# Decode attention with a fixed window: the second and third piece of the last values as a wide operand, and the output rows of heads 24 to 27 as 128-wide rows

## The chip, the core and the metric

The kernel runs on one core of a Trainium2 chip. The metric is the device time of one execution in microseconds (us). All times below are in microseconds unless marked ns, and times of events count from the start of the profiled span.

## The reference

Two branches start from the same layer-normed row `x` of 512 numbers. Branch A is one decode step of attention with 32 heads of 128 numbers; each head has keys and values of its own, of which the last 4096 positions are used. Branch B is a small MLP whose result gates branch A.

```python
xn = layernorm(x)
q = (xn @ wq) as 32 heads of 128
k, v = last 4096 positions of k_cache, v_cache       # 32 heads, bf16
p = softmax(q . k * 128 ** -0.5)
o = p @ v                                            # 32 x 128
s = o as 4096 @ wo                                   # 512
out = x + s * silu(B(xn))
```

Keys and values are 32 MB each (32 x 4096 x 128 in bf16), so about 79 MB are read for an output of 512 numbers.

## The kernel before

The heads go in eight groups of `G = 4` (`NG = 8`). A group's keys are one tile `kv` of 4 MB, and so are its values: 128 partitions, of which 32 belong to each head, and on every partition 128 "columns" (`CP`) of 128 numbers, one position each. The main loop runs `s` from 0 to 9. In step `s` it takes the scores of group `s` (part on VectorE, `k_vector`; part on TensorE, `k_turn` and `k_scores`), the softmax of the group before, and the values of group `h = s - 2` (`LAG`). Steps 8 and 9 have no keys any more: step 8 (`s == NG`) finishes the softmax of the last group and does the values of the seventh group; step 9 (the `else`) does the values of the eighth. TensorE, VectorE and ScalarE run in the order in which the code is written (`manual_schedule`). All large loads are issued from one queue in program order (`load`).

The values of a group are weighted in one of two ways:

- *Wide* (`v_wide`, L424): for every four columns one matmul with the 16 weights (4 columns x 4 heads) as the stationary operand and 512 numbers of values as the moving one. Four of these go side by side into four 32-row groups of the PSUM tile `ov`. Then ScalarE copies `ov` to `ov_sb` (L432), four transposes turn it into `ot_ps` (`v_turn`, L443), and VectorE adds up the wanted diagonal blocks into `oT` (`v_add`, L449): 128 numbers for each of the four heads.
- *Narrow* (`v_part`, L460): for each column one matmul with 128 x 128 values as the stationary operand and the four weights as the moving one, straight into `oT`. There is nothing to turn.

The last values arrive in four pieces, columns 0 to 63, 64 to 95, 96 to 111 and 112 to 127 (`cuts`). Behind them in the queue come the rows of `wo` for the last four heads, `wo_rows`, in three pieces: heads 28 and 29, head 30, head 31. In the kernel before, the first piece is wide and is turned at once; the other three are narrow, and add to the `oT` that `v_add` wrote.

`v_out` (L470 for the last groups) multiplies `oT` by the softmax's inverse denominators and gives `o` in bf16. The output projection splits the heads in blocks of 16, 8, 4 and 4. For the first three, `ox_spread` and `ox_pick` rearrange `o` to `ox`, so that a partition holds what fits its rows of `wo`. `y_wide` (L517) multiplies them with 512-wide rows of `wo` into `yr`, in four row groups whose partial sums ScalarE copies to `y_sum` (L640). `rows_add` (L153, its matmul is L156) then sums those into `y_ps`, which holds the 512 outputs as four rows of 128 numbers: it takes one matmul for each row, [...]. The last four heads go directly into `y_ps`, four 128-wide matmuls a head (`y_head`). Last come `y` (L650), `out_row` (L652) and the store.

Of the kernel before, what the change touches and what calls it, by code (L numbers as in the profile page):

```python
# [26 lines left out]
def kernel(  # L27
# [14 lines left out]
    nc = tc.nc  # L42
# [9 lines left out]
    CP = G * W // P  # L52
# [23 lines left out]
    def load(dst, src):  # L76
# [9 lines left out]
                        in_=A_wq.rearrange("(a b c) n -> b a (c n)", a=4, c=KC))  # L86
# [33 lines left out]
    ind = const.tile([P, 1], FP32, name="ind")  # L120
# [32 lines left out]
    def rows_add(ps, col, w, last):  # L153
        k = col.shape[0]
        for j in range(KC):
            nc.tensor.matmul(ps[32 * j:32 * j + 1, :], lhsT=col, rhs=w[0:k, j * P:(j + 1) * P],  # L156
                             start=False, stop=last, skip_group_check=True)
# [46 lines left out]
    for b in range(2):  # L204
        zeros(qr[b][:])
        for c in range(KC):
            wc = wq_sb[:, c, :].rearrange("p (g a d) -> p g a d", a=G, d=Dh)
            for a in range(G):
                nc.tensor.matmul(qr[b][32 * a:32 * a + 1], lhsT=xq_bf[:, c:c + 1], rhs=wc[:, 4 * b:4 * b + 4, a, :],  # L209
                                 start=False, stop=(c == KC - 1), skip_group_check=True)  # L210
    nc.scalar.copy(out=q_row[:, 0:4, 0, :], in_=qr[0][:])
    nc.vector.tensor_copy(out=q_row[:, 4:8, 0, :], in_=qr[1][:])  # L212
    for b in range(2):
        qb_ps = ps_tr.tile([P, 4, Dh], FP32, tag="pt", name="qb_ps")
        nc.tensor.matmul(qb_ps[:], lhsT=sel[:].rearrange("k b a -> k (b a)"), rhs=q_row[:, 4 * b:4 * b + 4, 0, :],
                         start=True, stop=True)
        nc.scalar.copy(out=q_bc[:, 4 * b:4 * b + 4, :], in_=qb_ps[:])
    for b in range(2):
# [5 lines left out]
        for t in range(2):  # L224
            rows = slice(64 * t, 64 * t + 64)
            nc.scalar.copy(out=q_pair[rows, 4 * b:4 * b + 4, :, G * t:G * t + G].rearrange("p g l a -> p g a l"),
                           in_=qt_ps[rows].bitcast(BF16).rearrange("p g (a m l) -> p g a m l", a=G, l=2)[:, :, :, 0, :])
# [4 lines left out]
    for j in range(KC):  # L232
        for c in range(KC):
            nc.tensor.matmul(hs_ps[:, j:j + 1], lhsT=w2_sb[:, c, j::4],
                             rhs=shifted_bf[:, c:c + 1], start=(c == 0), stop=(c == KC - 1))
# [30 lines left out]
    for i in range(11):  # L266
        n = P if i < 10 else 96
        terms.append((a_bf[0:n, i % 3, i // 3:i // 3 + 1], w4_sb[0:n, i, :]))
    for i, (col, w) in enumerate(terms):
        r = 32 * (i % 4)  # L270
        nc.tensor.matmul(hr_ps[r:r + 1].rearrange("r j n -> r (j n)"), lhsT=col, rhs=w, start=False,
                         stop=(i >= len(terms) - 4), skip_group_check=True)
# [124 lines left out]
    def sm_rden(g):  # L397
        s = st[g]
        s["rden"] = sm_pool.tile([P, G], FP32, tag="rden", name="rden")
        nc.vector.reciprocal(out=s["rden"][:], in_=s["den"][:])  # L400
# [20 lines left out]
    ov = ps_o.tile([P, 4, Dh], FP32, name="ov")  # L421
    zeros(ov[:])

    def v_wide(g, v, c1=CP):  # L424
        s = st[g]
        for i in range(c1 // 4):
            c, r = 4 * i, 32 * (i % 4)
            nc.tensor.matmul(ov[r:r + 4 * G], lhsT=s["pT"][:, c:c + 4, :].rearrange("p i a -> p (i a)"),  # L428
                             rhs=v[:, c:c + 4, :], start=(i < 4), stop=(i >= c1 // 4 - 4),
                             skip_group_check=True)  # L430
        s["ov_sb"] = sm_pool.tile([P, 4, Dh], FP32, tag="ov_sb", bufs=2, name="ov_sb")
        nc.scalar.copy(out=s["ov_sb"][:], in_=ov[:])  # L432

    def v_turn(g):
        s = st[g]
        if g == NG - 1:
            ot_ps = ps_tr.tile([P, 4 * P], FP32, tag="pt", name="ot_ps")
        else:
            ot_ps = ps_misc.tile([P, 4 * P], FP32, tag="misc", name="ot_ps")
        s["ot"] = ot_ps  # L440
        step = P - 4
        for j in range(4):
            nc.tensor.transpose(ot_ps[:, step * j:step * j + P], s["ov_sb"][:, j, :], ident_f[:])  # L443
# [13 lines left out]
    def v_part(g, v, c0, c1):  # L457
        s = st[g]
        for c in range(c0, c1):
            nc.tensor.matmul(s["oT"][:], lhsT=v[:, c, :], rhs=s["pT"][:, c, :], start=False,  # L460
                             stop=(c == CP - 1), skip_group_check=True)
# [23 lines left out]
    def ox_pick(i):  # L485
        n = blocks[i][1]
        to, mt, mh = masks[n]
        ox_ps = ps_misc.tile([P, n, n], FP32, tag="misc", name="ox_ps")
        nc.tensor.matmul(ox_ps[:], lhsT=to[:], rhs=ox_blk[i][:], start=True, stop=True)
        pick = sm_pool.tile([P, n, n], FP32, tag="pick", bufs=1, name="pick")  # L490
        nc.vector.tensor_tensor(out=pick[:], in0=ox_ps[:],
                                in1=mh[:].unsqueeze(2).to_broadcast([P, n, n]), op=ALU.mult)
        ox = sm_pool.tile([P, n], BF16, tag=f"ox{n}", bufs=1, name="ox")
        with nc.allow_low_precision("one nonzero addend, a bf16 value"):
            nc.vector.tensor_reduce(out=ox[:], in_=pick[:].rearrange("p h t -> p t h"), axis=AX.X,
                                    op=ALU.add)
        ox_blk[i] = ox
# [15 lines left out]
    def y_wide(i, last):  # L513
        n = blocks[i][1]
        for t in range(n):
            r = 32 * (t % 4)
            nc.tensor.matmul(yr[0][r:r + 1].rearrange("r j n -> r (j n)"), lhsT=ox_blk[i][:, t:t + 1],  # L517
                             rhs=wo_blk[i][:, t, :], start=False, stop=(last and t >= n - 4),
                             skip_group_check=True)

    def y_head(h):
        rows_add(y_ps, o_blk[3][:, h - h_part:h - h_part + 1], wo_row(h), h == H - 1)
# [7 lines left out]
    for s in range(NG + LAG):  # L530
        h = s - LAG
        last = h == NG - 1
        kn = load_kv(k_pool, A_k_cache, s, (0, 64, CP) if s == 0 else (0, CP)) if s < NG else None
        if s == LAG:
            wts_guard.__exit__(None, None, None)
            v_pool = ctx.enter_context(tc.tile_pool(name="v", bufs=V_BUFS))
            wo_blk[2] = v_pool.tile([P, 4, D], BF16, tag="wo_4", bufs=1, name="wo_4")
            wo_rows = v_pool.tile([P, H - h_part, D], BF16, tag="wo_rows", bufs=1, name="wo_rows")
        if last:
            v = load_kv(v_pool, A_v_cache, h, cuts)  # L540
            for r, n in ((H - G, 2), (H - 2, 1), (H - 1, 1)):
                load_rows(r, n)
        elif h >= 0:
            v = load_kv(v_pool, A_v_cache, h)
        if h == 3:
            wo_24 = k_pool.tile([P, 32, D], BF16, tag="kv", name="wo_24")
            wo_blk[0], wo_blk[1] = wo_24[:, 0:16, :], wo_24[:, 16:24, :]
            load_wo(0)
        if h == 5:
            load_wo(1)  # L550
            load_wo(2)

        if s < NG:
            nb = len(batches(s))

            def keys(b0, b1):
                for b in range(b0, b1):
                    k_turn(s, kn, b)
                    if b > 0:
                        k_scores(s, b - 1)  # L560

            k_open(s)
            k_vector(s, kn, 0)
            keys(0, 2)
            if s == 7:
                v_turn(h - 1)
                v_add(h - 1)
                v_out(h - 1)
            elif s > 1:
                sm_den(s - 2)  # L570
                sm_rden(s - 2)
            elif s == 1:
                sm_max(0)
            k_vector(s, kn, 1)
            keys(2, 4)
            if s == 7:
                sm_den(h)
                sm_rden(h)
                keys(4, nb - 2)
                sm_turn(s - 1)  # L580
                keys(nb - 2, nb)
            else:
                if s > 0:
                    sm_turn(s - 1)
                keys(4, nb)
            k_scores(s, nb - 1)
            sm_own(s)
            if s == 7:
                k_vector(s, kn, 2)
                v_wide(h, v)  # L590
                sm_exp(s - 1)
                v_turn(h)
                y_open()
                k_vector(s, kn, 3)
                v_add(h)
                v_out(h)
                ox_spread(1)
                sm_max(s)
                continue
            if s > 0:  # L600
                sm_exp(s - 1)
            if h > 0:
                v_turn(h - 1)
            k_vector(s, kn, 2)
            if h >= 0:
                v_wide(h, v)
            if h > 0:
                v_add(h - 1)
                v_out(h - 1)
            if s == 6:  # L610
                ox_spread(0)
            k_vector(s, kn, 3)
            if s == 6:
                ox_pick(0)
            if s > 0:
                sm_max(s)
        elif s == NG:
            ox_pick(1)
            sm_turn(NG - 1)
            sm_exp(NG - 1)  # L620
            y_wide(1, False)
            sm_den(NG - 2)
            sm_rden(NG - 2)
            y_wide(0, False)
            warm(3)
            v_wide(h, v)
            sm_den(NG - 1)
            sm_rden(NG - 1)
            v_turn(h)
            v_add(h)  # L630
            v_out(h)
            ox_spread(2)
        else:
            v_open(h)
            v_wide(h, v, cuts[1])
            ox_pick(2)
            v_turn(h)
            v_add(h)
            y_wide(2, True)
            nc.scalar.copy(out=y_sum[:], in_=yr[0][:].rearrange("p j n -> p (j n)"))  # L640
            v_part(h, v, cuts[1], cuts[2])
            rows_add(y_ps, ind, y_sum, False)
            for c0, c1 in zip(cuts[2:], cuts[3:]):
                v_part(h, v, c0, c1)
            v_out(h)
            for r in range(H - G, H):
                y_head(r)
# [36 lines left out]
```

## Time and profile before

| | |
|---|---|
| median time of 3 runs | 193.32 (193.32 to 193.47) |
| span of the profiled run | 191.1 |
| mean granted TensorE clock | 0.694 |
| VectorE busy | 150.9 (79% of the span) |
| TensorE matmul busy | 118.9 (62%) |
| ScalarE busy | 89.2 (47%) |
| moved by DMA | 79.02 MB, mean 413 GB/s |

The time is some 2 us longer than the span, which runs from the first to the last instruction. Busy times are sums over the whole span. Steps 8 and 9 are its last 20 us: from about 171 VectorE has no keys left to work on, and what remains are the last values, the output rows and the store.

In the timeline a line gives the start, the duration (first start to last end of what is merged), the engine, the line of code, the operation, what is written from what, shapes and the count; in brackets stands the idle time before it and what ended it. PEld is TensorE's loading of stationary operands. A line of the chain of waits gives start, duration and what the time went to; "issue" is time in which nothing that the profile shows was waited for. The table of stretches gives the busy time of PE, PEld, VectorE, ScalarE and GpSimd, and as its last three numbers the granted TensorE clock as a share of full speed, the busy share of the DMA engines, and GB/s.

### The profile page before, as it was taken

To read this page: it belongs to the slowest core of one execution; us is meant where nothing else is said; L and a number is where in the kernel's file an instruction comes from. 1 tells how busy PE (TensorE), PEld (TensorE's weight loads), DVE (VectorE), ACT (ScalarE), POOL (GpSimd) and SP (SyncE) were. 2 spreads that over 40 slices of the span, in tenths; PEclk is the share of its full clock that TensorE was granted. 3 is DMA by queue.
4 is the path that set the end of the run, shared out by engine and by line. 5 is a ranking of instruction groups with operands and counts; after the bars stand their busy time and mean duration, and the time that the engine had idled before them with its cause. 6 is when DMAs were issued, how large, how long until landed. Compare 5 with 4: busy or idle time off the path is not lost.

```text
span 191.1 us, 2883 instructions
## 1 busy us (share of the span) xinstructions
PE 118.9 (62%) x1180; PEld 76.2 (40%) x1180; DVE 150.9 (79%) x175; ACT 89.2 (47%) x191; POOL 2.3 (1%) x11
## 2 busy tenths in 40 slices
PE   1653854988734368256945773680989189739682
PEld 0430222767523334243434432540863078413351
DVE  1660159979999999999999999999999997990111
ACT  2001370887894076427464564542574147643120
POOL 2110000000000000000000000000000000000000
PEclk9999696555965557955575589558555855996965
DMA  6999999999999999999999999999999998999990
GB/s 211 447 425 413 427 429 429 439 439 430 439 434 439 439 429 425 439 439 432 422 432 425 439 422 408 442 439 435 439 432 441 435 439 372 485 432 387 413 367 26
DMA packets 4732, 79.02 MB, mean 413 GB/s; under 512 B 656, under 2 KB 1264, under 8 KB 1776
## 3 DMA queue, kind: packets, MB, share of 16 engines
q1 hardware_dynamic: 4424, 74.65, 91.5%
q10 hardware_dynamic: 296, 4.20, 5.2%
q8 instruction: 9, 0.15, 0.3%
q14 instruction: 3, 0.02, 0.0%
HBM read 78.84 MB, written 0.00 MB: 412 GB/s over the span
## 4 chain that ended last, share of the span: by engine, by line
DVE 47%; DMA 40%; PE 8%; ACT 1%; issue 1%; SPq 0%; DVEq 0%; ACTq 0%
DMA kv<-in_A_k_cache_dram 31%; DVE S L324 28%; DVE prod L322 16%; DMA kv<-in_A_v_cache_dram 7%; PE pt L340 3%; DMA x_bf<-in_A_x_dram 2%; PE ov L428 2%; ACT kt L343 1%; PE oT L460 1%; PE sT L351 1%; PE ot_ps L443 1%; DVE m L367 1%; DVE S L365 1%; PE y_ps L156 1%; DVE mx L375 1%
## 5 line engine op out<-in xcount | busy, mean ns | idle before, releaser
L324 DVE TENSOR_REDUCE S<-prod 128x20 f32<-128x2560 bf16 (+1 forms) x32 | 86.0, 2686 | 1.1
L343 ACT COPY kt<-pt 128x1024 bf16<-128x1024 bf16 x52 | 51.2, 1013 | 40.0 <-PE pt L340 38.2
L340 PE MATMUL pt<-ident_f,kv 128*128 128x128 f32 x208 | 47.4, 381 | 9.8 <-DMA kv<-in_A_k_cache_dram 9.8
L322 DVE TENSOR_TENSOR prod<-kv,q_bc 128x2560 bf16<-128x2560 bf16 (+1 forms) x32 | 45.4, 1418 | 3.3 <-DMA kv<-in_A_k_cache_dram 3.0
L340 PEld LDWEIGHTS pt<-ident_f,kv 128*128 128x128 f32 x208 | 34.8, 199 | 13.6 <-DMA kv<-in_A_k_cache_dram 9.3
L351 PE MATMUL sT<-q_pair,kt 128*128 128x8 bf16 x416 | 19.5, 171 | 15.4 <-ACT kt L343 15.3
L351 PEld LDWEIGHTS <-kt 128*128 128x128 bf16 x416 | 16.7, 105 | 26.3 <-ACT kt L343 25.3
L428 PE MATMUL ov<-kv,pT 128*16 128x512 bf16 x240 | 22.3, 536 | 1.5 <-DMA kv<-in_A_v_cache_dram 1.5
L432 ACT COPY ov_sb<-ov 128x512 f32<-128x512 f32 x8 | 4.7, 586 | 21.1 <-PE ov L428 21.1
L389 ACT ACTIVATE pT<-S,mb 128x128 bf16<-128x128 f32 x32 | 13.9, 572 | 0.3
L373 PE MATMUL mt_ps<-ident_f,m 128*1 128x128 f32 x8 | 2.8, 348 | 17.5 <-DVE rden L400 16.9
L428 PEld LDWEIGHTS <-pT 128*16 128x16 bf16 x240 | 6.6, 112 | 13.8 <-issue 12.2
L360 ACT ACTIVATE own<-sT,par 128x48 f32<-128x48 f32 (+1 forms) x32 | 7.5, 354 | 3.7 <-PE sT L351 3.7
L443 PE MATMUL ot_ps<-ident_f,ov_sb 128*128 128x128 f32 x32 | 7.6, 379 | 2.6 <-ACT mb L385 1.7
L212 DVE CAST q_row<-qr_ps 128x512 bf16<-128x512 f32 x1 | 0.7, 692 | 10.1 <-PE qr_ps L209 10.1
L389 ACT ACTIVATION_READ_ACCUMULATOR pT<-S,mb 128x1 f32 x32 | 8.2, 257 | 0.0
L373 PEld LDWEIGHTS mt_ps<-ident_f,m 128*1 128x1 f32 x8 | 0.6, 81 | 18.0 <-DVE rden L400 17.3
L400 DVE RECIPROCAL rden<-den_ps 128x4 f32<-128x4 f32 x8 | 1.4, 175 | 6.6 <-PE den_ps L395 6.6
L382 PE MATMUL mb_ps<-md,par_t 5*128 5x4 f32 x16 | 3.9, 309 | 4.4 <-DVE md L377 4.4
L443 PEld LDWEIGHTS ot_ps<-ident_f,ov_sb 128*128 128x128 f32 x32 | 4.8, 188 | 3.2 <-ACT mb L385 2.1
L256 ACT ACTIVATE a_row<-a_ps 128x384 bf16<-128x384 f32 x1 | 0.5, 490 | 12.0 <-remote 12.0
L209 PE MATMUL qr_ps<-wq_sb,xq_bf 128*1 128x512 bf16 x32 | 3.4, 607 | 3.7 <-DMA wq_sb<-in_A_wq_dram 3.7
(122 smaller groups left out, 83.7 us busy)
## 6 DMA issues: line engine op xcount, KB each, us to landing
kv<-in_A_k_cache_dram SPq DMA_DIRECT2D x7, 4096.0 KB, 29.1
kv<-in_A_v_cache_dram SPq DMA_DIRECT2D x7, 4096.0 KB, 30.7
wq_sb<-in_A_wq_dram ACTq DMA_DIRECT2D x1, 4096.0 KB, 17.5
kv<-in_A_k_cache_dram SPq DMA_DIRECT2D x2, 2048.0 KB, 25.4
wo<-in_A_wo_dram SPq DMA_DIRECT2D x1, 2048.0 KB
kv<-in_A_v_cache_dram SPq DMA_DIRECT2D x1, 2048.0 KB
w_sb<-in_B_w_dram SPq DMA_DIRECT2D x1, 1376.0 KB, 9.1
w_sb<-in_B_w_dram SPq DMA_DIRECT2D x1, 1280.0 KB, 19.3
```

What stands on the lines that cost most here:

```text
L209: nc.tensor.matmul(qr[b][32 * a:32 * a + 1], lhsT=xq_bf[:, c:c + 1], rhs=wc[:, 4 * b:4 * b + 4, a, :], start=False, stop=(c == KC - 1), sk ...
L322: nc.vector.tensor_tensor(out=prod[:, 0:m, :], in0=kn[:, rows, :], in1=q_bc[:, g:g + 1, :].to_broadcast([P, m, Dh]), op=ALU.mult)
L324: nc.vector.tensor_reduce(out=st[g]["S"][:, rows], in_=prod[:, 0:m, :], axis=AX.X, op=ALU.add)
L340: nc.tensor.transpose(pt[:, i, :], kn[:, c:c + 2, :].rearrange("p c d -> p (c d)").bitcast(FP32), ident_f[:])
L343: nc.scalar.copy(out=kts[b][:, 0:n, :], in_=pt[:, 0:n, :].bitcast(BF16))
L351: nc.tensor.matmul(st[g]["sT"][:, c:c + 2, :].rearrange("p c a -> p (c a)"), lhsT=kt[:, i, l::2], rhs=q_pair[:, g, l, :], start=(l == 0), ...
L360: nc.scalar.mul(s["own"][:, 0:m, a], s["sT"][:, 0:m, a], par[:, a:a + 1])
L382: nc.tensor.matmul(mb_ps[:], lhsT=par_t[:].rearrange("k b a -> k (b a)"), rhs=md[:], start=True, stop=True)
L389: nc.scalar.activation(out=s["pT"][:, :, a], in_=s["S"][:], func=ACT.Exp, scale=scale, bias=mb[:, a:a + 1], accum_out=s["sum"][:, a:a + 1])
L428: nc.tensor.matmul(ov[r:r + 4 * G], lhsT=s["pT"][:, c:c + 4, :].rearrange("p i a -> p (i a)"), rhs=v[:, c:c + 4, :], start=(i < 4), stop=( ...
L432: nc.scalar.copy(out=s["ov_sb"][:], in_=ov[:])
L443: nc.tensor.transpose(ot_ps[:, step * j:step * j + P], s["ov_sb"][:, j, :], ident_f[:])
```

## The change

`v_wide` takes a first column and may leave `ov` open. In the last step, the second and third piece of the values join the first as wide operands in `ov`, and the copy and the four transposes are made once, for columns 0 to 111. Only the fourth piece stays narrow. The output rows of heads 24 to 27 no longer go through `yr` but straight into `y_ps` as 128-wide rows (`y_rows`), two heads before the transposes and two behind the add. So `yr` is complete after the first two blocks, and its copy and sum move to step 8, the copy behind `y_wide(0)` and the sum behind the seventh group's values. This is meant to replace 48 narrow matmuls by 12 wide ones, and to take the copy and the sum out of the last step.

```diff
-    def v_wide(g, v, c1=CP):
+    def v_wide(g, v, c1=CP, c0=0, last=True):
         s = st[g]
-        for i in range(c1 // 4):
+        for i in range(c0 // 4, c1 // 4):
...
+        if not last:
+            return
         s["ov_sb"] = sm_pool.tile([P, 4, Dh], FP32, tag="ov_sb", bufs=2, name="ov_sb")
         nc.scalar.copy(out=s["ov_sb"][:], in_=ov[:])
...
+    def y_rows(t0, t1):
+        for t in range(t0, t1):
+            rows_add(y_ps, ox_blk[2][:, t:t + 1], wo_blk[2][:, t, :], False)
...
-            y_wide(0, False)
+            y_wide(0, True)
+            nc.scalar.copy(out=y_sum[:], in_=yr[0][:].rearrange("p j n -> p (j n)"))
             warm(3)
             v_wide(h, v)
             sm_den(NG - 1)
             sm_rden(NG - 1)
+            rows_add(y_ps, ind, y_sum, False)
             v_turn(h)
             v_add(h)
             v_out(h)
             ox_spread(2)
         else:
             v_open(h)
-            v_wide(h, v, cuts[1])
+            v_wide(h, v, cuts[1], last=False)
             ox_pick(2)
+            v_wide(h, v, cuts[3], cuts[1])
+            y_rows(0, 2)
             v_turn(h)
             v_add(h)
-            y_wide(2, True)
-            nc.scalar.copy(out=y_sum[:], in_=yr[0][:].rearrange("p j n -> p (j n)"))
-            v_part(h, v, cuts[1], cuts[2])
-            rows_add(y_ps, ind, y_sum, False)
-            for c0, c1 in zip(cuts[2:], cuts[3:]):
-                v_part(h, v, c0, c1)
+            y_rows(2, 4)
+            v_part(h, v, cuts[3], cuts[4])
             v_out(h)
             for r in range(H - G, H):
                 y_head(r)
```

More of the change, by code (lines that the diff above doesn't have):

```diff
@@ L422 @@
     zeros(ov[:])
-    def v_wide(g, v, c1=CP):
+    def v_wide(g, v, c1=CP, c0=0, last=True):
         s = st[g]
-        for i in range(c1 // 4):
+        for i in range(c0 // 4, c1 // 4):
             c, r = 4 * i, 32 * (i % 4)
             nc.tensor.matmul(ov[r:r + 4 * G], lhsT=s["pT"][:, c:c + 4, :].rearrange("p i a -> p (i a)"),
-                             rhs=v[:, c:c + 4, :], start=(i < 4), stop=(i >= c1 // 4 - 4),
+                             rhs=v[:, c:c + 4, :], start=(i < 4), stop=(last and i >= c1 // 4 - 4),
                              skip_group_check=True)
+        if not last:
+            return
         s["ov_sb"] = sm_pool.tile([P, 4, Dh], FP32, tag="ov_sb", bufs=2, name="ov_sb")
```

## The prediction

> **What bounds the kernel now.** I read the page's 40 slices first, then the end of the chain of waits, then the DMA issues of the last values one by one, and last the timeline of the tail.
>
> ```profile
> PEclk9999696555965557955575589558555855996965
> DMA  6999999999999999999999999999999998999990
> ```
>
> The transfers run at nine tenths in nearly every slice up to the last, so the end is set by what lands last and by the work that must follow it. The end of the chain:
>
> ```profile
> 167.36 13.78 DMA kv<-in_A_v_cache_dram
> ...
> 186.69 0.17 DVE o L470
> 186.87 0.04 issue
> 186.91 0.49 PE y_ps L156 x7
> 187.40 0.04 issue
> 187.44 0.30 PE y_ps L156 x4
> 187.74 0.02 issue
> 187.77 0.30 DVE y L650
> ```
>
> The first piece of the last values (columns 0 to 63) lands at 181.14 (167.36 + 13.78). The chain then names PE work only, yet it stops for 0.04 at 187.40. The timeline cut there shows why:
>
> ```profile
> 186.91 0.30 PEld L156 LDWEIGHTS <-o 128*1 128x1 bf16 x13 [0.34 <-DVE o L470]
> 186.91 0.49 PE L156 MATMUL y_ps<-wo_rows,o 128*1 128x128 bf16 x12 [0.25 <-DVE o L470]
> ```
>
> ```profile
> 187.44 0.27 PE L156 MATMUL y_ps<-wo_rows,o 128*1 128x128 bf16 x4
> 187.44 0.09 PEld L156 LDWEIGHTS <-o 128*1 128x1 bf16 x3 [0.23 <-issue]
> ```
>
> Thirteen weight loads but twelve matmuls had gone by then: the thirteenth matmul, the first of head 31, waited. The issues with their times to landing, each asked for in its own stretch, say for what (start, duration and count from the timeline; then size and landing):
>
> ```profile
> 168.59 1.24 SPq L77 DMA_DIRECT2D kv<-in_A_v_cache_dram  x2
> ...
> 171.03 0.43 SPq L77 DMA_DIRECT2D wo_rows<-in_A_wo_dram  x1
> ```
>
> ```profile
> kv<-in_A_v_cache_dram SPq DMA_DIRECT2D x1, 1024.0 KB, 15.6
> kv<-in_A_v_cache_dram SPq DMA_DIRECT2D x1, 512.0 KB, 16.2
> ...
> wo_rows<-in_A_wo_dram SPq DMA_DIRECT2D x1, 128.0 KB, 16.4
> ```
>
> The second piece (columns 64 to 95), issued at 167.95, lands at 167.95 + 15.6 = 183.55; the third (96 to 111) at 168.59 + 16.2 = 184.79; the fourth, issued at 169.23 with 16.8 to landing, at 186.03; the last output row (head 31) at 171.03 + 16.4 = 187.43. Its matmul starts at 187.44. So the old tail is as short as its transfers allow: only head 31's four matmuls (0.30) follow the last byte. Had o been ready 0.2 earlier, nothing would be gained. The slack is small too: the twelve matmuls of heads 28 to 30 need about 3 x 0.107 = 0.32 to be issued (the 0.107 is worked out below), so o may come 187.44 - 0.32 - 186.91 = 0.2 later at no cost.
>
> [...] the landings follow the issue order, 2.41 us apart for 1 MB and 1.24 for each half MB. [...] the clock turns between 183.0 and 184.0, as the next lines show, and it had risen at about 176.6, [...]. [...] Sixteen 512-wide ones took 1.04 at the full clock (timeline, 181.18), where one alone lasts 0.377.
>
> ```profile
> 182.50:183.00 0.50, 0.10 (x1) 0.10 (x2) 0.23 (x2) 0.35 (x1) 0.00 (x0) 1.00 0.99 410
> 183.00:183.50 0.50, 0.50 (x4) 0.32 (x4) 0.00 (x0) 0.00 (x0) 0.00 (x0) 0.90 0.96 393
> 183.50:184.00 0.50, 0.50 (x5) 0.09 (x4) 0.23 (x1) 0.00 (x0) 0.00 (x0) 0.50 0.98 395
> ```
>
> The third number from the end is the granted clock: half from 183.4 on. The old tail ran 3.2 us of PE work without a pause at that clock (183.53 to 186.67) and it stayed half to the end. The new tail has less PE work both before and after 183.4, so I take the half clock for all of it.
>
> **The change part by part.**
>
> *Row sum moved forward.* At step NG, the copy y_sum (0.58 on ScalarE) now follows the first blocks' last matmul (about 175.1); ScalarE is free from 174.4 to 178.42. The eight sum matmuls (0.61) stand before v_turn of the seventh group, which started at 179.06 when ov_sb came; they start at about 178.7 and push it by some 0.25. Behind it wait the DVE add, o and spread, done by 180.39 before, 180.65 now. The next user is ox_pick at 182.15, and the PE was waiting for the first piece until 181.18: cost nothing.
>
> *Taken out of the last step.* One ov_sb copy, four transposes and one DVE add after the first piece (182.27 to 183.87), four y_wide matmuls (0.60), the y_sum copy and its eight matmuls (0.61), and 48 narrow matmuls for columns 64 to 111. The PE had been busy with these from 183.53 to 186.67. All were hidden behind landings except in so far as they delayed o, and o was not what the end waited for.
>
> *Added: columns 64 to 95 as eight wide matmuls.* They start at 183.55 + 0.04. At half clock sixteen took 1.88 (y_wide at 173.21) and four took 0.60 (y_wide at 183.53), so a further one costs (1.88 - 0.60)/12 = 0.107, and eight 0.60 + 4 x 0.107 = 1.03. Done at 184.62, before the third piece at 184.79: hidden.
>
> *Added: columns 96 to 111 as wide, and only then the turn.* This is the cost. What used to be turned after the first piece, with 2.4 us to spare, is now behind the third. Step by step, each gap from the chain (0.04 DMA to PE at 181.14; 0.03 PE to ScalarE at 182.24; 0.04 ScalarE to PE at 182.86; 0.04 PE to DVE at 179.72; 0.04 DVE to PE at 186.87):
> - third piece 184.79, + 0.04 = 184.83;
> - four wide matmuls, 0.60 (half clock) to 185.43;
> - copy of ov, + 0.03 + 0.59 to 186.05;
> - four f32 transposes, + 0.04 + 1.09 (the same four at half clock, 155.62 in the timeline; 0.66 at full clock, 179.06) to 187.18;
> - DVE add, + 0.04 + 0.23 to 187.45;
> - sixteen narrow matmuls for the fourth piece (landed long before), + 0.04; 32 of them took 1.11, one 0.167, so 0.167 + 15 x 0.030 = 0.62 to 188.11;
> - o, + 0.02 + 0.17 to 188.30;
> - sixteen rows of heads 28 to 31, + 0.04; now without a wait: head 31's four took 0.30, a further head about 0.107 (four at 128 columns side by side; a quarter of the 512-wide group), 0.30 + 0.32 = 0.62 to 188.96.
>
> The old end of these rows was 187.74, so the tail grows by 1.22. y and out_row follow as before.
>
> *Heads 24-27 as 128-wide rows.* Sixteen matmuls into y_ps in place of four wide ones: two heads during the ScalarE copy (0.62 of idle PE against 0.30 + 0.107 = 0.41), two behind the transposes, during the DVE add. Two groups issued before 187.45 don't hold up the narrow ones. Their operand ox is ready at about 182.8 and wo_blk[2] was issued long before. Cost nothing, [...].
>
> Everything ahead of step NG is unchanged, so the issues from 167.36 to 171.03 and their landings stay. Sum: 193.32 + 1.2 = 194.5.
>
> **The rivals.**
> (A) *The clock is full in the tail.* Then 184.83 + 0.38 + 0.62 + 0.70 + 0.27 + 0.59 (narrow at 0.025, an estimate from the spacing of 0.027 to 0.030) + 0.19 + 0.04 and some 0.42 for the rows gives 188.04, 0.3 later than before: 193.6, hardly measurable. [...]
> (B) *The clock rises on the way*, [...]: narrow matmuls and rows faster, some 0.35 less, 194.1. [...]
> (C) *Less PE work is what counts, and the end comes sooner.* For it: the chain names PE from 181 to 187. Against: head 31's row lands at 187.43 whatever the PE does, so without a DMA that lands sooner the gain is nil; 193.3, or at best 193.0 if landings shift.
> (D) *Further waits,* [...] or a later third piece: + 0.4, 194.9.
>
> **How the numbers follow.** Half clock throughout 0.60 (194.5); B 0.14; A 0.13; C 0.05; D 0.08. The likeliest gives 194.5. The range reaches from A's 193.6 to D's 194.9. Slower by over 0.2% means above 193.71: half clock, B, D, nearly all: 0.82. Within 0.2%: A and part of C, 0.14. Faster: 0.04, the other part of C.
>
> **What would show it.** In the changed profile: the ov_sb copy of the last group near 185.4 in place of 182.27; the wait ahead of its four wide matmuls put down to the values' DMA; transposes lasting 1.09; o at about 188.1; sixteen rows in one run with no break; landings unchanged. Wrong if the third piece lands well before 184.8, if the clock stands at 1.0 after 183.4, or if o still comes before 187.1.

## Result, and the profile after

| | before | after |
|---|---|---|
| median time | 193.39 (193.23 to 193.97, 6 runs) | 194.45 (193.89 to 197.55, 6 runs) |
| ratio, 95% interval | | 1.0044 (1.0026 to 1.0062) |

The change makes the kernel about 1 us slower; 194.5 was predicted. Here and below the medians are of all runs, and the ratios leave out runs over 1.5% above the fastest of their kernel, as two of the six after the change (197.55 and the profiled one, 197.46). In that profile the transfers ran at 396 GB/s between 20 and 40 us, where the kernel before had 445, and everything behind came 2.9 later. So its tail is read from the landing of a piece onwards, not from the start of the span. The page:

```profile
PEclk9999588567555556955885579558555855996955
DMA  6998999999999999999999999999999999999970
```

In the last slice but one the transfers are now busy for seven tenths, where it was nine: a longer part of the end has none. The issues of the second and third piece, with start and time to landing:

```profile
170.84 0.60 SPq L77 DMA_DIRECT2D kv<-in_A_v_cache_dram  x1
...
171.49 0.59 SPq L77 DMA_DIRECT2D kv<-in_A_v_cache_dram  x1
```

```profile
kv<-in_A_v_cache_dram SPq DMA_DIRECT2D x1, 1024.0 KB, 15.6
kv<-in_A_v_cache_dram SPq DMA_DIRECT2D x1, 512.0 KB, 16.2
```

The times to landing are those of before, to the tenth. The third piece is there at 171.49 + 16.2 = 187.69. From there the timeline of the changed kernel's tail is:

```profile
186.50 1.03 PE L428 MATMUL ov<-kv,pT 128*16 128x512 bf16 x8 [1.29 <-DMA kv<-in_A_v_cache_dram]
...
187.73 0.60 PE L428 MATMUL ov<-kv,pT 128*16 128x512 bf16 x4 [0.20 <-DMA kv<-in_A_v_cache_dram]
...
188.11 0.44 PE L156 MATMUL y_ps<-wo,ox 128*1 128x128 bf16 x8
...
188.38 0.58 ACT L434 COPY ov_sb<-ov 128x512 f32<-128x512 f32 x1 [6.46 <-PE ov L428]
...
189.02 1.11 PE L445 MATMUL ot_ps<-ident_f,ov_sb 128*128 128x128 f32 x4 [0.47 <-ACT ov_sb L434]
...
190.07 0.38 PE L156 MATMUL y_ps<-wo,ox 128*1 128x128 bf16 x8
190.18 0.23 DVE L451 TENSOR_REDUCE oT<-ot_ps 128x4 f32<-128x64 f32 x1 [4.54 <-PE ot_ps L445]
...
190.46 0.57 PE L462 MATMUL oT<-pT,kv 128*128 128x4 bf16 x16
191.07 0.16 DVE L472 TENSOR_TENSOR o<-oT,rden 128x4 bf16<-128x4 f32 x1 [0.66 <-PE oT L462]
...
191.28 0.59 PE L156 MATMUL y_ps<-wo_rows,o 128*1 128x128 bf16 x16 [0.25 <-DVE o L472]
191.93 0.29 DVE L656 TENSOR_TENSOR y<-y_ps,g_row 128x128 f32<-128x128 f32 x1 [0.70 <-PE y_ps L156]
```

Read it as a chain. TensorE waits for the third piece, then ScalarE, TensorE, VectorE, TensorE, VectorE and TensorE follow one another, each waiting for the one before. In the kernel before, the same copy, turn and add lay ahead of the second piece's work. The break before head 31 is gone: all sixteen rows go in one run, since their transfers are long done (head 31's row landed at 190.24, `o` was ready at 191.23). From the third piece's landing to the end of the rows it is 191.91 - 187.69 = 4.22 (the chain of waits ends at 191.91); before it was 187.74 - 184.79 = 2.95. The clock in that stretch, from the table of stretches of the changed kernel (third number from the end):

```profile
183.00:186.00 3.00, 1.16 (x17) 0.49 (x17) 0.61 (x4) 0.00 (x0) 0.00 (x0) 1.00 0.96 400
186.00:187.20 1.20, 0.70 (x8) 0.24 (x8) 0.00 (x0) 0.00 (x0) 0.00 (x0) 0.61 1.03 414
187.20:191.00 3.80, 3.12 (x44) 1.62 (x39) 0.23 (x1) 0.58 (x1) 0.00 (x0) 0.50 0.54 196
```

### The profile page after: what moved, and what is told of

It reads as the page before. It is cut to its first block, busy times and chain, and to the rows that moved or that the text cites. A ratio compares the mean times of both kernels' runs of the same rounds, so it can differ in the third digit from the quotient of the medians.

```text
span 195.3 us, 2835 instructions
## 1 busy us (share of the span) xinstructions
PE 121.2 (62%) x1156; PEld 77.8 (40%) x1156; DVE 151.0 (77%) x175; ACT 89.6 (46%) x191; POOL 2.3 (1%) x11
## 4 chain that ended last, share of the span: by engine, by line
DVE 46%; DMA 42%; PE 7%; ACT 1%; issue 1%; SPq 1%; DVEq 0%
DMA kv<-in_A_k_cache_dram 32%; DVE S L324 27%; DVE prod L322 15%; DMA kv<-in_A_v_cache_dram 8%; PE pt L340 2%; DMA x_bf<-in_A_x_dram 2%; PE ov L428 1%; PE ot_ps L445 1%; ACT kt L343 1%; PE sT L351 1%; DVE m L367 1%; DVE S L365 1%; SPq L77 1%; DVE mx L375 1%; PE y_ps L156 0%
## 5 line engine op out<-in xcount | busy, mean ns | idle before, releaser
L340 PE MATMUL pt<-ident_f,kv 128*128 128x128 f32 x208 | 48.8, 389 | 10.9 <-DMA kv<-in_A_k_cache_dram 10.9
L340 PEld LDWEIGHTS pt<-ident_f,kv 128*128 128x128 f32 x208 | 35.8, 203 | 14.3 <-DMA kv<-in_A_k_cache_dram 9.9
L428 PE MATMUL ov<-kv,pT 128*16 128x512 bf16 x252 | 23.5, 531 | 2.9 <-DMA kv<-in_A_v_cache_dram 2.9
L451 DVE TENSOR_REDUCE oT<-ot_ps 128x4 f32<-128x64 f32 x8 | 1.7, 218 | 5.4 <-PE ot_ps L445 5.4
```

Source lines behind the costliest of these rows:

```text
L340: nc.tensor.transpose(pt[:, i, :], kn[:, c:c + 2, :].rearrange("p c d -> p (c d)").bitcast(FP32), ident_f[:])
```

## The experiments

Theory L says that only the late turn costs and that the old end was held by head 31's row. Its rivals: TensorE's work sets the end (W), or the moved rows and the moved sum cost (R). Ratios are to the kernel before in runs on the same chip, with the 95% interval.

| kernel | median | before | ratio |
|---|---|---|---|
| after_again | 194.81 | 193.32 | 1.0062 (1.0040 to 1.0084) |
| rows_only | 194.75 | 193.32 | 1.0059 (1.0039 to 1.0079) |
| merge_only | 193.89 | 193.32 | 1.0029 (1.0016 to 1.0041) |
| turn_at_96 | 193.65 | 193.32 | 1.0009 (0.9993 to 1.0025) |
| after_warm | 193.65 | 193.31 | 1.0033 (1.0017 to 1.0049) |
| before_warm | 193.35 | 193.31 | 1.0006 (0.9994 to 1.0018) |
| rows_again | 194.70 | 193.31 | 1.0050 (1.0029 to 1.0071) |
| rows_warm | 194.21 | 193.31 | 1.0039 (1.0018 to 1.0060) |
| before_pad | 193.37 | 193.24 | 1.0006 (0.9991 to 1.0021) |
| rows_trim | 193.32 | 193.24 | 1.0004 (0.9988 to 1.0019) |
| before_pad36 | 194.52 | 193.31 | 1.0063 (1.0044 to 1.0081) |
| before_no31 | 193.06 | 193.31 | 0.9986 (0.9976 to 0.9995) |

**The change once more (after_again).**

> The changed kernel once more, beside the others. Late turn (theory L): 1.0 to 1.2 us over the kernel before (ratio 1.005 to 1.006), and in the tail the rows of heads 28 to 31 end 4.1 to 4.2 us after the third piece of the last values lands, against 2.95 in the kernel before.

The chain held: in this profile, a run of 195.09, the third piece landed at 185.32 and the rows ended 4.21 later. The loss, 1.5 in the medians (of six runs, one of them 199.64), lies above the forecast; the ratio is at its upper end. The piece itself landed half a microsecond later than before, and one other run took as long (195.05). Without that half the run would be at 194.6, near the other three (194.23 to 194.57). Both profiles of the changed kernel have a slower stream early on (399 and 401 GB/s from 20 to 30 us, 445 in the kernel before), so none shows its tail with every piece on time.

**The wide operand alone (merge_only).** Against the kernel before:

```diff
-            v_wide(h, v, cuts[1])
+            v_wide(h, v, cuts[1], last=False)
             ox_pick(2)
-            v_turn(h)
-            v_add(h)
             y_wide(2, True)
             nc.scalar.copy(out=y_sum[:], ...)
-            v_part(h, v, cuts[1], cuts[2])
+            v_wide(h, v, cuts[3], cuts[1])
             rows_add(y_ps, ind, y_sum, False)
-            for c0, c1 in zip(cuts[2:], cuts[3:]):
-                v_part(h, v, c0, c1)
+            v_turn(h)
+            v_add(h)
+            v_part(h, v, cuts[3], cuts[4])
```

> The kernel before with the wide operand up to column 112 and one turn; the rows of heads 24 to 27 stay wide, with copy and row sum in the last step. Theory L: as slow as the changed kernel, 1.005 to 1.006, because the copy and the sum fit in the waits for the pieces and for the copy of ov. Theory R: as fast as before. Theory W: slower than the changed kernel by some 0.5 us, 1.008.

It is slower, but by half of what was expected. Its runs spread wider than those of the kernel before, roughly in two groups: twelve from 193.47 to 193.96 (median 193.66) and nine from 194.03 to 194.58 (median 194.41). The profiled run is of the lower one, and its timeline tells why that one is fast:

```profile
184.57 0.39 PE L428 MATMUL ov<-kv,pT 128*16 128x512 bf16 x4 [0.45 <-DMA kv<-in_A_v_cache_dram]
...
185.65 0.66 PE L445 MATMUL ot_ps<-ident_f,ov_sb 128*128 128x128 f32 x4 [0.47 <-ACT ov_sb L434]
...
187.42 0.39 PE L156 MATMUL y_ps<-wo_rows,o 128*1 128x128 bf16 x16 [0.25 <-DVE o L472]
```

Here TensorE's clock was full (1.00 in the table of stretches from 181 to 188): the turn takes 0.66 in place of 1.11, the rows 0.39 in place of 0.59. The third piece had landed at 184.53, and the rows ended at 187.84, 3.31 later: between the 2.95 of before and the 4.22 at half clock. At half clock the chain would be 0.9 longer by the 4.22 of the changed kernel, an estimate; the upper group lies 0.75 above the lower one, which fits, but no profile shows one of its runs.

**The turn one piece earlier (turn_at_96).** `v_wide(h, v, cuts[2], cuts[1])` in place of `cuts[3]`, third and fourth piece narrow.

> The changed kernel with the turn after the second piece (column 96), third and fourth piece narrow. Theory L: the turn starts behind eight wide matmuls after 183.55, so o comes at about 188.0 and the rows end at 188.6: 0.9 us over the kernel before (1.0045), 0.3 less than the changed kernel. If only the waiting for the third piece cost, it would be near the kernel before.

The forecast missed: on the whole it is as fast as the kernel before. Two groups again: eight runs from 193.15 to 193.79 and four from 194.05 to 194.23. In the profiled run, of the lower group, the clock was full (1.00 from 181 to 187; the turn took 0.66):

```profile
184.83 0.66 PE L445 MATMUL ot_ps<-ident_f,ov_sb 128*128 128x128 f32 x4 [0.57 <-ACT ov_sb L434]
...
187.00 0.20 PEld L156 LDWEIGHTS <-o 128*1 128x1 bf16 x13 [0.34 <-DVE o L472]
187.01 0.71 PE L156 MATMUL y_ps<-wo_rows,o 128*1 128x128 bf16 x16 [0.26 <-DVE o L472]
187.49 0.09 PEld L156 LDWEIGHTS <-o 128*1 128x1 bf16 x3 [0.29 <-issue]
```

Thirteen weight loads, then a pause, then three: head 31 waits for its row as in the kernel before, so the late turn is hidden and the time is that of before. This also answers R for these rows: the moved sum, the 128-wide rows and eight wide matmuls are all in this kernel, and here they cost nothing that shows (0.5 at most by the interval). The upper group lies 0.8 above the kernel before, near the 0.9 of the sum at half clock; but five of the 34 runs of the kernel before lie at 194.06 to 194.19 too, so it need not be the clock.

**The clock held up (after_warm, before_warm).** In after_warm, `warm(5)` stands ahead of the first and of the second piece, and `warm(2)` ahead of the third; before_warm has the first of them.

> The changed kernel with matmuls on zeros in the waits for the pieces (five ahead of the first piece, five ahead of the second, two ahead of the third), so that TensorE's clock stays at full in the tail. They write a PSUM tile that nobody reads. Clock theory (the size of the loss is the half clock on the chain behind the third piece): transposes 0.67 in place of 1.11, rows 0.42 in place of 0.62, 0.3 us over the kernel before (1.0015 to 1.002), with few runs above 194.0. If the clock didn't matter: as the changed kernel, 1.005 to 1.006.

> The kernel before with five matmuls on zeros ahead of the first piece. Its end is held by the landing of head 31's row, so a full clock brings nothing: 0.999 to 1.001. If TensorE's work in the last step set the end, 0.3 to 0.6 us faster.

Twelve of eighteen runs of after_warm lie from 193.51 to 193.73, 0.3 above the kernel before as expected; six lie from 194.39 to 194.99, more than the few that were expected above 194.0. The profiled run is one of these six. Its clock was 1.00 from 180 to 189, and it still shows the short chain:

```profile
186.58 0.66 PE L445 MATMUL ot_ps<-ident_f,ov_sb 128*128 128x128 f32 x4 [0.57 <-ACT ov_sb L434]
...
188.36 0.39 PE L156 MATMUL y_ps<-wo_rows,o 128*1 128x128 bf16 x16 [0.26 <-DVE o L472]
```

In that run the third piece landed only at 185.46, and the rows ended 3.32 behind it. The lateness is the stream's (390 GB/s from 25 to 30 us, against 449), not the tail's; the other five have no profile.

The kernel before gains nothing by a full clock (ratio 1.0006), as it should if the landing holds its end. That speaks against W. Its profile, with a turn of 0.66, names the landing:

```profile
187.52 0.23 PE L156 MATMUL y_ps<-wo_rows,o 128*1 128x128 bf16 x4 [0.16 <-DMA wo_rows<-in_A_wo_dram]
```

**The rows alone (rows_only, rows_again, rows_warm, rows_trim).** The last step of the changed kernel with the turn at column 64, as before, and `y_rows(0, 4)` behind the add.

> The changed kernel with the wide operand ended at column 64 again and turned there, as before; the row sum in step 8 and the 128-wide rows stay. Theory L (only the late turn costs, and the old end is held by the landing of head 31's row): same as before, 0.999 to 1.001, o ready up to 0.7 us earlier and head 31 still waiting for its row. Theory W (TensorE's work in the last step sets the end): 0.4 to 0.7 us faster, 0.997. Theory R (the rows or the moved row sum cost): slower by 0.3 us or more.

> The kernel with only the rows and the row sum moved, once more, for a profile of an undisturbed run. If its loss of 1.3 us was a slower stream between 20 and 50 us, as the first profile shows, then with a full stream in that stretch it is as the kernel before, 193.2 to 193.4, with head 31 waiting for its row. If the rows or the moved sum cost something, its tail behind the third piece's landing is longer than the 2.95 of the kernel before.

This was a surprise: 1.4 slower, where L said nothing and W said faster. Only R had forecast a loss. It is not the stream: in the profile of rows_again that ran at 437 GB/s from 20 to 30 us. The profile has head 31's rows waiting 1.31 us:

```profile
187.27 0.49 PE L156 MATMUL y_ps<-wo_rows,o 128*1 128x128 bf16 x12 [0.25 <-DVE o L472]
189.07 0.28 PE L156 MATMUL y_ps<-wo_rows,o 128*1 128x128 bf16 x4 [1.31 <-DMA wo_rows<-in_A_wo_dram]
```

```profile
wo_rows<-in_A_wo_dram SPq DMA_DIRECT2D x1, 128.0 KB, 18.6
```

18.6 to landing, where it was 16.4 before: not the rows' matmuls but their transfer. The trace has the moment at which each of the 16 DMA engines finished its part of that row: fifteen by 187.70, the sixteenth at 189.03. What kept it stands in the DMA list for 186.9 to 188.4:

```profile
q8 instruction: 1, 0.02, 4.0%
```

One packet of 16 KB of instructions, 0.96 us long, from 187.04 to 188.00. Of the data packets 44 began after it did: 39 by 187.40, and the last five one after another from 187.99, as it ended. So by these times one engine kept its last packets of the row behind the instructions. R is right that this kernel is slower, but what it waits for is a transfer, not the rows' matmuls or the sum.

There are nine such packets a run, of 16 KB and 0.88 to 1.32 us each in the profiled runs. In rows_again it is the ninth that came ahead of the row's last packets on one engine, which ended the row 1.33 after the other fifteen.

The theory F from this: the more instructions TensorE has ahead of that point, the earlier the ninth fetch comes. That the packets hold TensorE's instructions is part of the theory: the DMA list names no engine for them. The first kernels to test it were rows_warm (five more matmuls) and rows_trim (sixteen fewer, the rows of heads 24 to 27 left out).

> The same with five matmuls on zeros ahead of the first piece of the last step, which also makes the program a little longer. If the edit of the rows itself cost 1.3 us, this is as slow as the first run of it (1.006). If it is a chance of that run or of the program's placement, 0.999 to 1.001, with the rows of head 31 waiting for their landing.

> The kernel with only the rows moved, less the sixteen matmuls of the rows of heads 24 to 27, which are left out of the output: 1176 matmuls, fewer than the kernel before. Theory F: the fetch comes behind head 31's row again, 193.2 to 193.4 in most runs. If the moved row sum cost, 194.5 to 194.9 stays. (If the sixteen matmuls themselves cost 1.4 us, this run is fast too; the padded kernel before tells that apart.)

rows_warm was as the kernel before in six of its runs, at 193.9 in two and at 194.5 or more in eight; rows_trim lost its delay (eleven of thirteen runs from 193.07 to 193.56). rows_trim fits F but doesn't prove it. rows_warm does not follow from the number of instructions alone: it has more than rows_again, yet only half of its runs are slow. In its profile (193.89) the five matmuls kept TensorE from the first piece until 182.42, 0.7 after its landing, and the fetch, at 187.63, held no packet.

**The instruction fetch by itself (before_pad, before_pad36).** The kernel before, with 12 or 36 matmuls on zeros ahead of the first piece, meant for an idle stretch of TensorE:

```diff
+            pad(36)
             v_wide(h, v, cuts[1])
```

where `pad(n)` is n times

```python
nc.tensor.matmul(wm[:, 0, 0:G], lhsT=zero_bf[:], rhs=zero_bf[:, 0:G], start=True, stop=True)
```

> The kernel before with twelve tiny matmuls (128 x 4, on zeros, into a tile nobody reads) in the PE's idle time ahead of the first piece of the last values: 1192 matmuls, as many as the kernel with only the rows moved. Theory F (the ninth 16 KB instruction fetch, which comes as TensorE nears the end of its program, gets ahead of head 31's row on one DMA engine when the program has more instructions before that point): about 1.4 us slower, 194.5 to 194.9 in most runs, and head 31's row lands over 1 us after the other rows, on one engine. Theory R (the rows or the moved sum cost by themselves): as before, 193.2 to 193.4.

> The kernel before with 36 tiny matmuls on zeros (72 instructions) in the PE's idle time ahead of the first piece, three times the first pad. Theory F: the ninth instruction fetch comes earlier still, ahead of head 31's packets on its DMA engine, and most runs are at 194.5 to 194.9. If the number of PE instructions is not what brings the fetch forward, most runs stay at 193.2 to 193.4, as with twelve.

Twelve were not enough, against F's forecast (193.37; thirteen of seventeen runs below 193.5); thirty-six cost 1.2 us in the median and over 0.9 in every run (194.26 to 195.26). In the latter's profile the fetch began at 184.71, and it was the fourth piece of the values that came late on one engine:

```profile
187.58 0.58 PE L460 MATMUL oT<-pT,kv 128*128 128x4 bf16 x16 [1.40 <-DMA kv<-in_A_v_cache_dram]
```

From the records of single packets and landings, one profiled run each:

```
kernel        matmuls  9th fetch  packets begun after it  head 31's row on 15 / on 16 engines
after           1156    189.76            4                  190.19 / 190.24
before          1180    187.01            2                  187.31 / 187.39
before_pad      1192    186.84            6                  187.19 / 187.26
rows_trim       1176    186.98            2                  187.32 / 187.37
after_again     1156    187.64            0                  187.91 / 188.06
rows_again      1192    187.04           44                  187.70 / 189.03
before_pad36    1216    184.71              481              187.29 / 188.78
```

In the kernel before, the fetch starts just as the last data are through: it is on the edge. The changed kernel has 24 matmuls fewer, and in its two profiles the fetch starts just as close to the last data (four packets and none begun after it) and holds none of them.

That a fetch which comes ahead of the last data costs a microsecond is shown, by the 36 (1.2 in the median) and by the held packets of rows_again (head 31's row 1.33 late on one engine). That the number of instructions sets the fetch is not. In rows_again it started when it did in the kernel before (187.04 and 187.01), but the data were later: its third piece landed at 185.15, not 184.79. With the twelve of before_pad it came 2.26 after the third piece's landing, as in the kernel before (2.22), and in rows_again 1.89 after it. In the profile of before_pad the twelve did not fall into idle time either: they ran from 181.30 to 181.74, and the first piece had landed at 180.93. Why rows_only meets the fetch in most runs and before_pad, with as many matmuls in all, in few, is not settled. In rows_only the narrow matmuls run ahead of where they were before and then wait for the fourth piece, so that TensorE may reach the same instruction earlier; that is only argued.

**Head 31 left out (before_no31).** Load and row of head 31 are not there.

> The kernel before without head 31's output row: its load and its four matmuls are left out, so head 31 is missing from the output. If the landing of that row sets the end (theory L), the end moves to o and the three other heads' rows: 12 matmuls after 186.91, 0.49, so 187.4 in place of 187.74, 0.3 us faster (0.998 to 0.999). If TensorE's chain sets it, 0.1 us or less (four matmuls at 0.027).

0.25 faster (0.10 to 0.46 by the interval), on L's side. The profile has the twelve remaining rows in one run behind `o`; it is of a run of 193.19 in which the pieces landed 0.3 later than before, so the gain itself is seen in the median alone:

```profile
187.25 0.42 PE L156 MATMUL y_ps<-wo_rows,o 128*1 128x128 bf16 x12 [0.25 <-DVE o L470]
187.72 0.29 DVE L650 TENSOR_TENSOR y<-y_ps,g_row 128x128 f32<-128x128 f32 x1 [0.52 <-PE y_ps L156]
```

No version beat the kernel before with the whole output computed.

## Why the prediction was right

- *The old end is held by head 31's landing.* Right. Taking work off TensorE (rows_trim) and a full clock (before_warm) brought nothing; taking the row away brought 0.25, where 0.3 was expected.
- *Eight wide matmuls behind the second piece are hidden.* Right: 1.03 predicted, 1.03 measured, 0.20 of wait left before the third piece.
- *The chain behind the third piece.* Right in every term: four wide 0.60 (0.60), copy 0.59 (0.58), turn 1.09 (1.11), add 0.23 (0.23), narrow 0.62 (0.57), o 0.17 (0.16), rows 0.62 (0.63 in the chain of waits); in sum 4.17 predicted from the landing to the end of the rows, 4.22 measured. The chain grew by 1.27 (1.22 predicted) and the median by 1.06, in after_again by 1.5; that 194.45 lies within 0.1 of the forecast is in part luck.
- *The 128-wide rows and the moved sum lie beside other work.* Right in the changed kernel: eight rows from 188.11 to 188.55, about the start of ScalarE's copy, and eight beside the VectorE add. The sum's matmuls (eight in the trace, for four rows in f32) ran from 181.52 to 181.92 and didn't push the turn at 181.97, where 0.25 was allowed.
- *The clock.* The half clock was the likeliest case for this kernel, and both its profiles have it. But its reason, that the clock stays at half with less TensorE work, was an assumption of the prediction and does not carry: merge_only has fewer matmuls still (1144) and was at full clock in its profile, as was turn_at_96 (1168). Of the eleven profiles without added `warm`, five had the half clock at the last rows and six the full one. So the half clock in both profiles of the changed kernel was in part luck, and rival A deserved more than 0.13. By their times nearly all runs of the changed kernel look like half clock; one, at 193.89, may be at full, but it has no profile. How busy TensorE was in these stretches does not settle it either: in the kernel before it was busy for 3.25 of 3.40 us from 183.4 to 186.8, and the clock stayed at half (0.50) to the end; in turn_at_96 it was busy for 2.07 of 3.00 from 184 to 187, at 1.00. What sets the clock is not shown.
- *Missing from the prediction:* that instructions are themselves a transfer on the same DMA engines (nine packets of 16 KB in the profile of before and in that of the changed kernel). In the two profiles of the changed kernel no fetch held a packet, and of its other runs it is not known; but it made "cost nothing" for the moved rows untrue once they stood alone.

Open: why the stream between 20 and 30 us was slower in five profiled runs (388 to 401 GB/s in the change, after_again, rows_only, after_warm and rows_warm; 419 in before_no31) than in the others (437 to 451). That part of the program is the same in all.

## What to carry to other kernels

When pieces of an operand arrive one by one, a step with a fixed latency (a copy, a turn, an add across three engines; 0.58, 1.11 and 0.23 in the changed kernel) belongs behind an early piece, and what comes last should need the shortest chain, even where it takes more instructions. Before counting the work that an edit takes away, find what the last wait is for: here it was a transfer, and 12 matmuls in place of 48 bought nothing. And a gain or loss of a microsecond at the very end of a stream can come from where an instruction fetch falls (1.33 on head 31's row in rows_again), so before it is put down to an edit, see whether the last load is late on all DMA engines or on one. A pad of as many idle instructions did not tell it here.

## What the runs showed of the hardware that was not expected

- A 16 KB instruction packet took 0.88 to 1.32 us on its DMA engine. Head 31's row is split over 16 engines and landed with the slowest: in rows_again fifteen ended it by 187.70 and one at 189.03, 1.33 later, with an instruction packet of 0.96 ahead of its last packets.
- The 16 engines of one load drifted apart in the kernel before. They ended a load within 0.45 at 25.5 us; in the load after the first instruction fetch (28.4) one was 1.38 behind the next, and stayed so in the load after that; in the third piece of the last values ten of the sixteen were 1.4 to 2.0 behind the first. That each such step is an instruction packet is not shown.
- Half the clock did not double the times: four f32 turns of 128 x 128 took 1.11 in the changed kernel and 0.66 in merge_only, four 512-wide matmuls in four column groups 0.60 and 0.39, sixteen 128-wide rows 0.59 and 0.39.
